# Two chunks of w3 and of w_out per weight tile, and tiles moved by 32 bytes, in a fused attention and two-MLP kernel

## The chip, the cores and the metric

The kernel runs on one core of a Trainium2 chip. The metric is the device time of one execution in microseconds (us). Three executions before the change took 1218.69, 1219.29 and 1219.76 us; the median, 1219.29 us, is what the change is measured against.

## The reference

Attention with four batches, eight heads, 768 positions and head size 64, where a position sees the first 8 keys and the last 96; its result goes through two MLPs without a pause:

```python
scores = scale * np.matmul(q, k.transpose(0, 1, 3, 2))
scores = np.where(keep, scores + bias, -1e9)       # keep: local 96 or global 8
a = softmax(scores); x = np.matmul(a, v)           # -> x: 3072 x 512
h = ((x @ w1) * (x @ w2)) @ w3                     # 512 -> 1024 -> 1024
x = h @ w_out                                      # -> 512
h = x @ w_in                                       # 512 -> 2048
out = (h * np.cos(h)) @ w_out2                     # -> 3072 x 512
```

All of it is float32. The weights reach the device as 8-byte words that the kernel has to decode.

## The kernel before

**Three stages.** First, w3 and w_out are multiplied into one matrix W = w3 @ w_out, in 16 slots `c` (two halves `h`, eight chunks `k`). Second, eight blocks `j` of 384 tokens run attention, up (`up`: x by w1 and by w2) and down (`down`: the product by W), in twelve slots each. Third, six steps `J` of 512 tokens run the second MLP: `hidden` (x by w_in), `gate` (h cos h) and `project` (by w_out2), sixteen chunks `m` per step.

**Order.** It is written by hand (`manual_schedule`): every engine runs its instructions in the order of the code, and waits by semaphores where a tile is not ready or not free.

**Decoding.** Each chunk of 128x512 weights is loaded as `raw` by SyncE, turned into float by ScalarE (`dec_words`: one pass into the chunk's tile, one into `s`), and put together by VectorE (`dec_shift`, `dec_sign`, `dec_sum`). A chunk of w3 or w_out is decoded straight into a tile of the pool `wts`, under the tag `Wb` (four buffers) for w3 and `wB` (eight) for w_out. A buffer there has 4096 bytes per partition, since later tiles (`W`, `wA`, `wB`: a high and a low part of 512 floats) need that much; a chunk fills 2048 of them. In the profile the chunks are `w` and `wo`.

**A slot of the first stage** interleaves the chunk's four matmuls (`wmm`, L835) with attention of unit `n = c - 2`: scores (L529), values of unit n - 2 (`x_ps`, L621), transposes of unit n - 1 (`pt_ps`, L594 and L596), their copy by ScalarE (`pt`, L604 or L609), which the values of the next slot read, the exponentials (`e`, L568), and decoding steps in between. ScalarE's order in a slot is: a chunk of w3 (`w`, `s`), the copy `pt`, other decoding, the exponentials.

**Matmuls of the second and third stage** are made of three: the high part of the stationary operand by the high and by the low part of the moving one, then the low part by the high one (`mm3`, L384 to L386). Each one loads its stationary operand anew. In a name such as `mm<-xT,wA` the moving tile stands first, the stationary one second.

```python
nc.tensor.matmul(ps, lhsT=l_hi, rhs=r_hi, start=first and i == 0, stop=False)
nc.tensor.matmul(ps, lhsT=l_hi, rhs=r_lo, start=False, stop=False)
nc.tensor.matmul(ps, lhsT=l_lo, rhs=r_hi, start=False, stop=last and i == n - 1)
```

The moving operand has 384 columns in `up` and `down` (`xT` by `wA` or `wB`; `ab` by `W`), 512 in `hidden` (`x2in` in even steps J, `x2in_b` in odd ones, by chunks of w_in in `wA`, `wB`, `wC`) and 512 in `project` (chunks of w_out2 in `wB`, `Wa`, `Wb`, and for the last two chunks `wD`, by `g`). Scores of later units (L537, L541) have 232 columns: per head, the stationary q of `hh` by k of `hh` and by the low part `kl`; the second head's k and `kl` begin 928 bytes behind the first one's.

**Where tiles begin.** Pools on the left side grow from low addresses, those on the right side down from the end of a partition. The program's allocation puts the tiles that matmuls read at these bytes of a partition, modulo 512 (all further steps inside a tile are multiples of 512, save the 928 above and 256 in `v`):

| tile | side | before | after |
|---|---|---|---|
| `W`, `wA`, `wB`, `Wa`, `Wb`, `wC`, `x2in` | left | 192 | 192 |
| `hh` (two buffers) | left | 448, 256 | 448, 256 |
| `kl` (two buffers), behind `st` | left | 224, 32 | 320, 128 |
| `pt`, behind `st` | left | 288 | 384 |
| `v` | left | 64 | 64 |
| `xT`, `ab`, `g`, `x2in_b`, `wD` | right | 480 | 448 |

Before, three `st` tiles of 16 bytes, 32 apart, push what follows them on the left by 96 bytes, and the right side ends 32 bytes off a multiple of 64. So before, all tiles of the right side and `kl` and `pt` begin at 32 modulo 64, the rest at 0.

Of the kernel before, what the change touches and what calls it, by code (L numbers as in the profile page):

```python
# [8 lines left out]
F32 = mybir.dt.float32  # L9
# [253 lines left out]
def fused(ctx, tc, a_qk, a_v, w3p, wo1p, w1p, w2p, winp, wo2p, n_global, n_local, out):  # L263
    nc = tc.nc

    def pool(name, bufs, side="left", space=None):
        kw = {} if space is None else {"space": space}
        if space is None:
            kw["side"] = side
        return tc.alloc_tile_pool(name=name, bufs=bufs, reuse_waits="tile", **kw)  # L270
# [2 lines left out]
    x2s = dram.tile([MO, 128, 2, NT], F32R, name="x2s")  # L273
    late_w = dram.tile([2, M2, 128, 512], F32, name="late_w")

    misc = pool("misc", 1)
    wts = pool("wts", 8)
    attn = pool("attn", 2)
# [14 lines left out]

    raws, xs, ss, wt = {}, {}, {}, {}

    rings, taken = {}, {}

    def ring(key, tag, shape, dt):  # L300

        pools = rings[key][tag]
        i = taken[tag] = taken.get(tag, -1) + 1
        at = i % sum(n for _, n in pools)
        for p, n in pools:
            if at < n:
                return p.tile(shape, dt, tag=tag, name=tag, bufs=n)
            at -= n
# [5 lines left out]
    def dec_words(key):  # L314
        r = raws[key]
        if key[0] in ("w3", "wo1"):
            tag = dest[key]
            kw = {"bufs": 4} if tag == "Wb" else {}
            x = xs[key] = wts.tile([128, 512], F32, tag=tag, name=key[0], **kw)
        else:  # L320
            x = xs[key] = ring(key, "x", [128, 512], F32)
        nc.scalar.activation(x, r[:, :, 1].bitcast(F32), ACTF.Copy, scale=2.0 ** -112)
        ss[key] = ring(key, "s", [128, 512], I32)
        nc.scalar.activation(ss[key], r[:, :, 0].bitcast(U32), ACTF.Copy, scale=2.0 ** -29)
# [147 lines left out]
    def where(n):  # L472
        j, r = divmod(n, UPB)
        p, i = divmod(r, TPB)
        return j, p, i, (TPB * j + i) % (S // 128)

    plain = {}
    qk_raw, v_raw, hh, kl, es, sts, pts, xps, xT = {}, {}, {}, {}, {}, {}, {}, {}, {}
# [67 lines left out]
    def a_max(n):  # L546

        if not 0 <= n < NU:
            return
        _, p, _, t = where(n)  # L550
        w = WIN if t else 128
        bias = bias1 if t else bias0
        es[n] = attn.tile([128, 2, WIN], F32, tag="e", name="e", bufs=2)
        sts[n] = attn.tile([128, 2, 2], F32, tag="st", name="st", bufs=3)
        sp = s_ps.pop(n)
        for e in range(2):
            nc.vector.tensor_tensor_reduce(  # L557
                out=es[n][:, e, :w], in0=sp[:, e, :w], in1=bias[:, 2 * p + e, :],
                scale=-0.125, scalar=3.0e38, op0=ALU.add, op1=ALU.min,
                accum_out=top[:, n, e:e + 1],  # L560
            )
# [170 lines left out]
    with tc.manual_schedule():  # L732
# [8 lines left out]
        for o in "3A3A3A3A3A3A3A3ABBBBBBBB":  # L741
# [3 lines left out]
            else:  # L745
                n, m = ups.pop(0)
# [16 lines left out]
        def decoder():  # L763
# [5 lines left out]
            for i in range(n + 5):  # L769
# [13 lines left out]
                if k[0] and fast:  # L783
                    dec_words(k[0])
# [20 lines left out]
                if k[0] and not fast:  # L805
                    dec_words(k[0])
# [22 lines left out]
        for c, (h, k) in enumerate(chunks):  # L829
            n = c - 2  # L830
# [25 lines left out]
            if n >= 0:  # L856
                a_load_plain(n + 2)
            a_values(n - 2)
            a_max(n)
            decode(1)  # L860
            a_out(n - 2)
# [21 lines left out]
        w2p_ = None  # L883
# [7 lines left out]
        for j in range(NB1):  # L891
            for i in range(UPB):
                sl = j * UPB + i
                n = sl + LEAD
                last = j == NB1 - 1
                if last and i == 0:
                    attn.release()
                    w2p_ = pool("w2p", 6)
# [14 lines left out]
                if 1 <= i <= M1:  # L913
                    up_mult(j, i - 1)
                    up_hi(j, i - 1)
                a_max(n)
                decode(3 if sl < 8 else sl % 2)
                if i == 0 and j > 0:
# [34 lines left out]
        p2 = pool("p2", 2, side="right")  # L953
        p_h = pool("p_h", 4, space=PSUM)
        p_o = pool("p_o", 4, space=PSUM)
# [15 lines left out]
        def gate(J, m, meanwhile=iter(())):  # L971
            ps = h_ps.pop((J, m))
            kt = p2.tile([128, TB2], I32, tag="kt", name="kt")
            r = p2.tile([128, TB2], F32, tag="r", name="r")
            nc.scalar.activation(kt, ps, ACTF.Identity, scale=INV2PI)  # L975
            next(meanwhile, None)
            nc.vector.scalar_tensor_tensor(  # L977
                out=r, in0=kt, scalar=-C1, in1=ps, op0=ALU.mult, op1=ALU.add
            )
            nc.vector.scalar_tensor_tensor(  # L980
                out=r, in0=kt, scalar=-C2, in1=r, op0=ALU.mult, op1=ALU.add
            )
            next(meanwhile, None)
            nc.scalar.activation(r, r, ACTF.Sin, scale=0.5)  # L984
            run(meanwhile)
            nc.vector.scalar_tensor_tensor(  # L986
                out=r, in0=r, scalar=-2.0, in1=r, op0=ALU.mult, op1=ALU.mult
            )
            nc.vector.scalar_tensor_tensor(  # L989
                out=r, in0=r, scalar=1.0, in1=ps, op0=ALU.add, op1=ALU.mult  # L990
            )
            t = g[J, m] = p2.tile([128, 2, TB2], F32R, tag="g", name="g", bufs=3)
            nc.scalar.copy(out=t[:, 0, :], in_=r)  # L993
            nc.vector.tensor_tensor(  # L994
                out=t[:, 1, :], in0=r, in1=t[:, 0, :].bitcast(F32), op=ALU.subtract
            )
# [25 lines left out]
        for s in range(len(steps) + LAG):  # L1022
# [14 lines left out]
            if s < len(steps):  # L1037
                if J == 0 and m < 5:
                    tag = ("Wa", "Wa", "Wb", "Wb", "wD")[m]
                    gate(J, m, late_split("o2", 3 + m, tag, p2 if m == 4 else None))  # L1040
                else:
                    gate(J, m)
        for p in (p_o, p_h, p2, w2p_, wts):
            p.release()


# [78 lines left out]
```

## Time and profile before

| | before |
|---|---|
| median of three executions | 1219.29 us |
| the profiled execution | 1223.8 us |
| its span, first to last instruction | 1222.0 us |
| TensorE (PE) busy | 1169.2 us, 96% |
| weight loads (PEld) busy | 988.9 us, 81% |
| VectorE (DVE) busy | 770.5 us, 63% |
| ScalarE (ACT) busy | 579.0 us, 47% |
| mean granted TensorE clock | 0.986 |

Busy times are shares of the whole span, and the three stages differ: the rows further down give stretches. Ends of matmuls are modelled, so that a matmul's pace is read from the distance between the starts of two, not from its duration.

### The profile page before, as it was taken

What the parts mean: (1) busy time and instruction counts of PE and PEld (TensorE: products, weight loads), DVE (VectorE), ACT (ScalarE), POOL (GpSimd) and SP (SyncE); (2) the same over time, 40 slices, a digit from 0 to 9 for tenths busy, and PEclk for the clock granted to TensorE, in tenths of its full rate; (3) what the DMA queues carried; (4) which work ended last, traced back from release to release, by engine and by line L of the source; (5) the groups of instructions that cost most, each with busy time, mean ns of one, the idle gap of its engine ahead of it and who ended that gap; (6) DMA issues with size and microseconds to landing.
All of it is one profiled execution on the core that took longest, in us unless ns stands there. A gap on an engine that the chain in (4) does not pass through costs nothing.

```text
span 1222.0 us, 17352 instructions
## 1 busy us (share of the span) xinstructions
PE 1169.2 (96%) x6178; PEld 988.9 (81%) x6178; DVE 770.5 (63%) x1756; ACT 579.0 (47%) x1256; POOL 124.3 (10%) x213
## 2 busy tenths in 40 slices
PE   4889789999999999999999999999999999999997
PEld 1334678999999999999999888878888888888885
DVE  7578987666667654555534566666666666665664
ACT  5457766666666555555534433333333333333332
POOL 0000122111111111111114200000000000000000
PEclk8889999999999999999999999999999999999998
DMA  8646578565464423334146321201102002000001
GB/s 251 206 153 213 189 267 266 167 186 190 136 214 156 152 87 121 109 100 123 45 138 202 109 68 28 77 1 48 57 1 69 35 1 70 35 1 21 15 1 37
DMA packets 65295, 132.72 MB, mean 109 GB/s; under 512 B 6576, under 2 KB 27184, under 8 KB 65200
## 3 DMA queue, kind: packets, MB, share of 16 engines
q1 hardware_dynamic: 58672, 118.95, 30.3%
q0 software_dynamic: 6528, 12.58, 3.5%
q8 instruction: 50, 0.82, 0.3%
q14 instruction: 45, 0.37, 0.1%
HBM read 104.25 MB, written 27.26 MB: 108 GB/s over the span
## 4 chain that ended last, share of the span: by engine, by line
PE 87%; DVE 4%; ACT 3%; DMA 3%; issue 2%; POOL 0%; SPq 0%; ACTq 0%; DVEq 0%; POOLq 0%
PE mm L384 11%; PE mm L385 10%; PE mm L386 10%; PE o_ps L386 7%; PE o_ps L384 7%; PE h_ps L384 7%; PE h_ps L386 7%; PE o_ps L385 7%; PE h_ps L385 7%; PE x_ps L621 4%; PE mm L835 3%; PE pt_ps L594 2%; PE s_ps L541 1%; PE s_ps L537 1%; PE pt_ps L596 1%
## 5 line engine op out<-in xcount | busy, mean ns | idle before, releaser
L585 POOL TENSOR_SCALAR e<-e,st 128x232 f32<-128x232 f32 (+1 forms) x164 | 84.0, 525 | 528.7 <-DVE st L581 181.0
L984 ACT ACTIVATE r<-r 128x512 f32<-128x512 f32 x96 | 60.7, 632 | 153.5 <-DVE r L980 153.5
L993 ACT CAST g<-r 128x512 fp32r<-128x512 f32 x96 | 59.6, 621 | 139.5 <-DVE r L989 139.5
L505 ACT CAST hh<-qk 128x720 fp32r<-128x720 f32 x82 | 65.0, 793 | 117.2 <-PE s_ps L541 104.7
L986 DVE SCALAR_TENSOR_TENSOR r<-r 128x512 f32<-128x512 f32 x96 | 66.5, 692 | 70.5 <-ACT r L984 70.4
L994 DVE TENSOR_TENSOR g<-r,g 128x512 fp32r<-128x512 f32 x96 | 66.5, 693 | 66.0 <-ACT g L993 66.0
L384 PE MATMUL mm<-xT,wA 128*128 128x384 f32 x256 | 92.3, 361 | 0.0
L384 PE MATMUL mm<-xT,wB 128*128 128x384 f32 x256 | 92.0, 360 | 0.0
L384 PE MATMUL mm<-ab,W 128*128 128x384 f32 x256 | 91.5, 358 | 0.1
L568 ACT ACTIVATE e<-e,top 128x232 f32<-128x232 f32 (+1 forms) x192 | 89.3, 467 | 3.7 <-DVE top L557 3.7
L557 DVE CUSTOM_DVE_ANT_0 e<-s_ps,bias 128x232 f32<-128x232 f32 (+1 forms) x192 | 65.4, 377 | 38.5 <-PE s_ps L541 36.1
L977 DVE SCALAR_TENSOR_TENSOR r<-kt,h_ps 128x512 f32<-128x512 int32 x96 | 65.7, 684 | 33.5 <-ACT kt L975 33.4
L385 PE MATMUL mm<-xT,wA 128*128 128x384 f32 x256 | 86.8, 339 | 0.0
L386 PE MATMUL mm<-xT,wB 128*128 128x384 f32 x256 | 86.8, 339 | 0.0
L386 PE MATMUL mm<-xT,wA 128*128 128x384 f32 x256 | 86.7, 339 | 0.0
L385 PE MATMUL mm<-xT,wB 128*128 128x384 f32 x256 | 86.7, 339 | 0.0
L385 PE MATMUL mm<-ab,W 128*128 128x384 f32 x256 | 86.2, 337 | 0.2 <-DVE ab L671 0.2
L386 PE MATMUL mm<-ab,W 128*128 128x384 f32 x256 | 86.1, 336 | 0.0
L621 PE MATMUL x_ps<-pt,v 128*64 128x128 f32 (+1 forms) x704 | 59.8, 286 | 25.2 <-ACT pt L604 20.5
L835 PE MATMUL mm<-wo,w 128*128 128x512 f32 x128 | 70.1, 681 | 12.8 <-DVE wo L340 12.8
L664 DVE TENSOR_TENSOR ab_f<-mm,a_sb 128x384 f32<-128x384 f32 x64 | 35.6, 556 | 68.0 <-PE mm L386 65.3
L975 ACT ACTIVATE kt<-h_ps 128x512 int32<-128x512 f32 x96 | 57.3, 596 | 39.6 <-PE h_ps L386 39.6
(189 smaller groups left out, 3032.3 us busy)
## 6 DMA issues: line engine op xcount, KB each, us to landing
qk<-in_a_qk SPq DMA_DIRECT2D x82, 360.0 KB, 3.2
v<-in_a_v SPq DMA_DIRECT2D x97, 128.0 KB, 2.1
x2s<-x2t SPq DMA_DIRECT2D x32, 384.0 KB, 3.0
raw<-in_w3p SPq DMA_DIRECT2D x16, 512.0 KB, 4.5
raw<-in_winp SPq DMA_DIRECT2D x16, 512.0 KB, 4.3
late_w<-x SPq DMA_DIRECT2D x32, 256.0 KB, 2.2
raw<-in_wo2p SPq DMA_DIRECT2D x16, 512.0 KB, 4.1
raw<-late_w SPq DMA_DIRECT2D x16, 512.0 KB, 4.6
```

Of the source, the lines that this page charges most:

```text
L384: nc.tensor.matmul(ps, lhsT=l_hi, rhs=r_hi, start=first and i == 0, stop=False)
L385: nc.tensor.matmul(ps, lhsT=l_hi, rhs=r_lo, start=False, stop=False)
L386: nc.tensor.matmul(ps, lhsT=l_lo, rhs=r_hi, start=False, stop=last and i == n - 1)
L505: nc.scalar.copy(out=hh[n], in_=qk_raw[n])
L557: nc.vector.tensor_tensor_reduce(out=es[n][:, e, :w], in0=sp[:, e, :w], in1=bias[:, 2 * p + e, :], scale=-0.125, scalar=3.0e38, op0=ALU.ad ...
L568: nc.scalar.activation(es[n][:, e, :w], es[n][:, e, :w], ACTF.Exp, bias=top[:, n, e:e + 1], scale=-1.0, accum_out=sts[n][:, 0, e:e + 1],)
L585: (engine or nc.gpsimd).tensor_scalar(es[n][:, e, :w], es[n][:, e, :w], st[:, 1, e:e + 1], 1.0, ALU.mult, ALU.mult)
L621: nc.tensor.matmul(x[e * 64:(e + 1) * 64, i * 128:(i + 1) * 128], lhsT=vt[:kk, c, e * 64:(e + 1) * 64], rhs=pt[:kk, e, c, :], start=c == 0 ...
L835: nc.tensor.matmul(W_ps[m], lhsT=wt["w3", c][:, m * 128:(m + 1) * 128], rhs=wt["wo1", k], start=k == 0, stop=k == M1 - 1,)
L977: nc.vector.scalar_tensor_tensor(out=r, in0=kt, scalar=-C1, in1=ps, op0=ALU.mult, op1=ALU.add)
L986: nc.vector.scalar_tensor_tensor(out=r, in0=r, scalar=-2.0, in1=r, op0=ALU.mult, op1=ALU.mult)
L994: nc.vector.tensor_tensor(out=t[:, 1, :], in0=r, in1=t[:, 0, :].bitcast(F32), op=ALU.subtract)
```

## The change

Two edits. Chunks 2i and 2i + 1 of w3, and of w_out, become the two halves of one tile of 4096 bytes. And two tiles are made larger or added for their size alone: `st` grows from 16 to 64 bytes, and a pool `edge` takes 32 bytes at the end of the right side, so that all tiles in the table above begin at multiples of 64 bytes.

```diff
+    edge = pool("edge", 1, side="right")
+    edge.tile([128, 8], F32, name="edge")
     misc = pool("misc", 1)
     wts = pool("wts", 8)
...
         if key[0] in ("w3", "wo1"):
             tag = dest[key]
             kw = {"bufs": 4} if tag == "Wb" else {}
-            x = xs[key] = wts.tile([128, 512], F32, tag=tag, name=key[0], **kw)
+            if key[1] % 2 == 0:
+                two[key[0]] = wts.tile([128, 2, 512], F32, tag=tag, name=key[0], **kw)
+            x = xs[key] = two[key[0]][:, key[1] % 2, :]
...
-        sts[n] = attn.tile([128, 2, 2], F32, tag="st", name="st", bufs=3)
+        sts[n] = attn.tile([128, 8, 2], F32, tag="st", name="st", bufs=3)
```

No instruction changes its place on any engine; what changes is what some of them wait for. On ScalarE, in the slots where the first scores are already under way (`w` is a chunk of w3, `wo` one of w_out; a wait named PE is for a matmul, DMA for a load), it reads before:

```order
31 L322 ACTIVATE w_320<-raw 128x512 [waits DMAHW4_49,PE_49]
32 L324 ACTIVATE s<-raw 128x512 [waits DVE_49,Activation_49]
33 L568 ACTIVATE e,st<-e,top 128x232 [waits DVE_49] x2
34 L609 COPY pt<-pt_ps 128x2x128
35 L322 ACTIVATE wo_355<-raw 128x512 [waits DMAHW7_49]
36 L324 ACTIVATE s<-raw 128x512 [waits Activation_49]
37 L322 ACTIVATE w_367<-raw 128x512 [waits DMAHW0_49,PE_49]
```

The same place after the change (the code stands seven lines further down):

```order
31 L329 ACTIVATE w_275<-raw 128x512 [waits DMAHW4_49]
32 L331 ACTIVATE s<-raw 128x512 [waits DVE_49,Activation_49]
33 L575 ACTIVATE e,st<-e,top 128x232 [waits DVE_49] x2
34 L616 COPY pt<-pt_ps 128x2x128 [waits PE_49]
35 L329 ACTIVATE wo_306<-raw 128x512 [waits DMAHW7_49]
36 L331 ACTIVATE s<-raw 128x512 [waits Activation_49]
37 L329 ACTIVATE w_363<-raw 128x512 [waits DMAHW0_49]
```

The wait for a matmul is gone from the chunks of w3, twelve of the sixteen having had one; the copy `pt` now names its own wait for the transposes, which the chunk ahead of it used to cover.

## Rows read from the trace of the kernel before

**Rows 1.** Windows: length, busy us of each engine (instructions), granted clock, DMA share, GB/s.

```profile
20.00:103.00 83.00, 64.98 (x208) 31.03 (x206) 57.32 (x176) 44.77 (x105) 0.00 (x0) 0.88 0.61 185
103.00:210.00 107.00, 94.11 (x556) 78.28 (x556) 92.40 (x244) 78.23 (x180) 17.07 (x22) 0.97 0.73 242
210.00:678.60 468.60, 468.38 (x3101) 444.27 (x3100) 265.97 (x790) 256.95 (x642) 85.32 (x157) 1.00 0.45 143
678.60:1211.00 532.40, 532.40 (x2300) 430.65 (x2299) 339.83 (x506) 186.71 (x310) 20.68 (x25) 1.00 0.11 35
```

**Rows 2.** Waits, 30 to 104 us: us in total, times, longest.

```profile
ACT w L322 <- PE mm L835: 30.0, 10, 5.2
...
DVE st L578 <- ACT e L568: 12.9, 4, 4.7
...
PE x_ps L621 <- ACT pt L604: 7.7, 5, 2.7
...
PE x_ps L621 <- ACT pt L609: 4.6, 3, 2.4
```

**Rows 3.** Chain that ended last, inside one slot: start, length, what.

```profile
88.80 1.73 PE mm L835 x4
...
90.56 0.70 ACT w L322
91.25 0.56 ACT s L324
91.82 0.26 ACT pt L609
...
92.12 0.44 PE x_ps L621 x4
```

**Rows 4.** Timeline, PE, hidden with x2in: third and last matmul of twelve.

```profile
885.33 0.39 PE L386 MATMUL h_ps<-x2in,wA 128*128 128x512 f32 x1
...
887.37 0.40 PE L386 MATMUL h_ps<-x2in,wA 128*128 128x512 f32 x1
```

**Rows 5.** The same with x2in_b; first of hidden, first and last of project.

```profile
962.41 0.39 PE L384 MATMUL h_ps<-x2in_b,wC 128*128 128x512 f32 x1
...
965.21 0.40 PE L384 MATMUL o_ps<-wB,g 128*128 128x512 f32 x1
...
967.78 0.40 PE L386 MATMUL o_ps<-wB,g 128*128 128x512 f32 x1
```

**Rows 6.** The same, project with wD: two starts six matmuls apart.

```profile
1208.65 0.39 PE L386 MATMUL o_ps<-wD,g 128*128 128x512 f32 x1
...
1210.01 0.39 PE L386 MATMUL o_ps<-wD,g 128*128 128x512 f32 x1
```

**Rows 7.** Timeline, PE: second and last of twelve in down, then one unit's scores.

```profile
400.34 0.34 PE L385 MATMUL mm<-ab,W 128*128 128x384 f32 x1
...
402.07 0.34 PE L386 MATMUL mm<-ab,W 128*128 128x384 f32 x1
402.25 0.27 PE L537 MATMUL s_ps<-hh 128*128 128x232 f32 x1
402.35 0.28 PE L541 MATMUL s_ps<-kl,hh 128*128 128x232 f32 x1
402.46 0.27 PE L537 MATMUL s_ps<-hh 128*128 128x232 f32 x1
402.58 0.27 PE L541 MATMUL s_ps<-kl,hh 128*128 128x232 f32 x1
```

**Rows 8.** Windows of two whole steps: J = 2 with x2in, J = 3 with x2in_b.

```profile
851.73:940.14 88.41, 88.41 (x386) 72.07 (x384) 56.08 (x82) 30.19 (x51) 2.84 (x5) 1.00 0.12 36
940.14:1029.61 89.47, 89.47 (x385) 72.07 (x384) 56.05 (x82) 30.18 (x51) 2.85 (x5) 1.00 0.12 36
```

**Rows 9.** Groups of PE, 210 us to the end: one of nine alike.

```profile
L385 PE MATMUL mm<-xT,wA 128*128 128x384 f32 x224 | 75.4, 336 | 0.0
```

**Rows 10.** One window at the lower granted clock in the first stage.

```profile
44.80:48.20 3.40, 3.40 (x9) 1.74 (x8) 3.17 (x10) 0.10 (x1) 0.00 (x0) 0.50 0.79 241
```

More of the change, by code (lines that the diff above doesn't have):

```diff
@@ L288, in fused @@
     pt_ps = p_t.tile([128, 2, 2, 128], F32, name="pt_ps")
-    raws, xs, ss, wt = {}, {}, {}, {}
+    raws, xs, ss, wt, two = {}, {}, {}, {}, {}
     rings, taken = {}, {}
@@ L1042, in fused @@
                     gate(J, m)
-        for p in (p_o, p_h, p2, w2p_, wts):
+        for p in (p_o, p_h, p2, w2p_, wts, edge):
             p.release()
```

## The prediction

> **What bounds the kernel now.** I read the windows of the stages first, then the waits of the first stage, then the distances between matmul starts in the other two. In [rows 1] TensorE is busy for 468.38 of 468.60 us in the second stage and for all of 532.40 us in the third, at the full granted clock: from 210 us to the last matmul it is the bound, and what counts there is how far apart it starts its matmuls. From 103 to 210 us VectorE, with 92.40 of 107 us, is the fullest; TensorE waits at times. From 20 to 103 us nobody is full: TensorE 64.98 of 83 us, VectorE 57.32, ScalarE 44.77. There the reader should see a ring. ScalarE waits 30.0 us, ten times, with a chunk of w3 for a matmul (L835) to free the buffer [rows 2]. Behind that chunk stand, on ScalarE, `s` and then the copy `pt`, for which the values of the next attention unit wait: the chain runs from four matmuls (1.73 us) through `w` (0.70), `s` (0.56) and `pt` (0.26) back to TensorE [rows 3]. TensorE's idle time before the values, put down to `pt`, is 7.7 + 4.6 = 12.3 us, and VectorE's before `st`, put down to the exponentials that also stand behind the chunk, 12.9 us [rows 2].
>
> **The change: chunks in pairs.** Four buffers hold eight chunks instead of four, so a chunk no longer waits for the matmuls of the chunk four before it; all ten waits go. Nothing is added to any engine. ScalarE then runs the chunk as soon as its load has landed. Most that this can give is the 12.3 us in which TensorE stands still for it, since its remaining time in the stretch is work. What is late next? VectorE: it is busy 57.32 of 83 us, and inside a slot the exponentials wait for its maxima and the transposes for its normalised rows. TensorE's 65 us and VectorE's 57 us must interleave in order, slot by slot, and a slot holds about 5.5 us of either; with 18 us of slack for TensorE to begin with, I do not expect all of it back. Bounds: 2 us, if VectorE or the loads take the place of nearly every wait, and 12.3 us; to the upper one may come the clock: a mean of 0.88 over 83 us [rows 1] means some 20 us at 1.2 GHz, in pieces such as the 3.4 us at 0.50 of [rows 10], and if half of those 20 us ran at 2.4 GHz where TensorE stands still less, that would give back up to 5 us more. I take 9 us, nearer to the upper bound, because VectorE, which is next in line, itself stood 12.9 us for the same exponentials [rows 2] and comes forward with them. From 103 us VectorE bounds the same work in the same order, so the 9 us arrive there early and stay early.
>
> **The change: beginnings.** The trace of before already has both cases. With `x2in`, which begins at 192 like its stationary chunks, nine distances take 887.37 - 885.33 = 2.04 us, 226.7 ns each [rows 4]. With `x2in_b`, at 480 against 192, twelve take 965.21 - 962.41 = 2.80 us, 233.3 ns each; and in `project`, with the moving chunk at 192 and the stationary `g` at 480, eleven take 2.57 us, 233.6 ns [rows 5]. It isn't the 480 as such: with `wD` and `g`, both at 480, six take 1.36 us, 226.7 ns again [rows 6]. So what costs is that the two operands differ by 32 modulo 64: 6.6 to 6.9 ns a matmul of 512 columns. Two whole steps say the same: with 192 matmuls of the matching kind instead of the other, J = 2 is 89.47 - 88.41 = 1.06 us shorter than J = 3, 5.5 ns each [rows 8].
>
> After the change all these tiles begin at 0 modulo 64. Third stage: 576 matmuls of `hidden` on `x2in_b` (3 steps, 16 chunks, 12 each) and 1008 of `project` (6 steps, 14 chunks, 12 each; the two chunks in `wD` already match). At 6.2 ns, between the 5.5 of whole steps and the 6.9 of inner distances, that is 1584 x 6.2 = 9.8 us.
>
> Second stage: six groups of 224 and three of 228 matmuls of 384 columns stand after 210 us [rows 9], 2028 in all, every one with its moving tile (`xT`, `ab`) at 480 against 192; none of this width matches anywhere, so its price is bounded. One run has ten distances in 402.07 - 400.34 = 1.73 us, 173 ns [rows 7]; over the stage the inner distances average 174.6 ns. Below: scores of 232 columns, first head, match, and go 0.10 us to the next [rows 7] (105 ns over 81 units); the straight line from there to 226.7 ns at 512 columns gives 105 + 152 x 0.435 = 171 ns at 384, a gain of 3.5 ns (nothing but 2 ns if that one run were typical). Above: the 6.6 ns of 512 columns, and where 232 columns do not match the next start is 0.11 to 0.12 us off (112 and 113 ns over the units), 7 to 8 ns more, so the loss doesn't shrink with width. I take 5 ns, between the two: 10.1 us, with 4 to 13.4 for the range. The 276 earlier ones stand where VectorE is the bound and count nothing.
>
> Scores: `kl` of the first head now matches (82 units by 7 ns, 0.6 us gained); `kl` of the second head, 928 bytes on, matched before and no longer does, but what follows it is not another such matmul but the values, which wait for their own copy, so I cost that at nothing; if it counts, it takes the 0.6 us back. The larger `st` and the new pool move no instruction and add none.
>
> At this place a rule speaks against the change. The Trainium skill, "TensorE: Matmul & The Clock Gate", section "Step-by-step: what each phase is for", says that TensorE has two independent read ports, one for the moving operand and one for weight loads, so that loading the next weights takes nothing from the running matmul. By it no beginning could matter and this part's gain would be nothing; rows 4 to 6, at 226.7 against 233.6 ns, disagree. The trace decides, and I give the rule's outcome to a rival below.
>
> **The sum.** 9 + 9.8 + 10.1 + 0.6 = 29.5 us. The profiled execution took 1223.8 us (span 1222.0), so it would take 1194.3; the median of the three runs lies 4.5 us under the profiled one, and I forecast a median of **1190 us**.
>
> **Rivals.** (1) Beginnings pay, pairs don't: ScalarE's wait for the matmul is replaced by one for a load or for VectorE. For it: VectorE is busy for 57.32 us of 83, the DMA share is 0.61, and loads stand in SyncE's queue behind loads of `v` that wait for the values. Against: VectorE itself waited for the exponentials. 20.5 us without the 9, of which 2 may stay: 1197 to 1199 us. (2) Pairs pay, beginnings don't: the offset that costs is not 32 but any difference below 512, and after the change the right side still stands 256 off the left one (448 against 192). Every pair that was slow had the 32 in its difference, every fast one had a difference of 0, so the trace has no pair that is 256 off alone. Against: differences of 288 and of 224 (rows 5) cost the same within 0.3 ns, so the larger bits seem to do nothing. 1219.3 - 9, 1210 us. The rule of the Trainium skill quoted above, from "TensorE: Matmul & The Clock Gate", would give the same time. (3) Neither: 1219 us, within 0.2%, which is about what a measurement of this kernel can tell from no change. (4) Slower: 256 off costs more than 32 did. It would bite in the second and third stage, at some 3600 matmuls; from 2.5 ns on top of today's each it outweighs the 9 us of the pairs, and at twice today's loss (6.6 more, 3612 x 6.6 = 24 us) the time is 1234 us. Against it stands the same 0.3 ns.
>
> **Chances and range.** Both parts pay, 1181 to 1198 us: 0.70. Rival 1: 0.12. Rival 2: 0.12. Rival 3: 0.03. Rival 4: 0.03. The forecast's own bounds: least 2 + 8.7 + 4 = 15 us (1584 x 5.5 = 8.7), most 12.3 + 10.9 + 13.4 + 0.6 + 5 for the clock = 42; both ends at once are unlikely, and 1180 to 1206 us holds rival 1 and most of the first case, with a little of rival 2: 8 in 10. Faster by over 0.2%: 0.94; same: 0.03; slower: 0.03.
>
> **What would show it.** Pairs: ScalarE's wait for L835 before a chunk of w3 gone from the waits; TensorE's idle time before the values between 20 and 103 us down from 12.3 to about 3 us; the second stage's full part beginning 9 us sooner. Beginnings: a step J of 87.3 us, odd or even; 226.7 ns inside runs of `hidden` and of `project`; about 169 to 170 ns inside `up` and `down`. Wrong it would be if the distances stay at 233 and 174 ns (the 256), if ScalarE stands before the same chunks for another releaser, or if TensorE, quicker by 3%, begins to stop in the second stage for VectorE, which has 266 of 468.6 us of work there.

## The result, and the profile after

Four executions of the changed kernel took 1187.69 to 1192.95 us, median **1191.43 us**, beside 1218.99 us (1217.78 to 1219.76) for the kernel before on the same chip: a ratio of 0.977, 95% interval 0.9746 to 0.9794. The forecast said 1190 us. The profiled execution took 1191.22 us, its span is 1189.4 us, 32.6 us below that of before; by medians the gain is 27.6 us, since the profiled execution of before stood 4.8 us over the median given here and the one of after does not. What follows compares the two profiled executions.

Line numbers are higher by seven in after (L842 for L835, L391 to L393 for L384 to L386). The windows of the stages, with the columns of [rows 1] and the borders moved to where the third stage now begins:

```profile
20.00:103.00 83.00, 78.17 (x294) 38.90 (x293) 75.79 (x229) 60.77 (x140) 0.00 (x0) 0.96 0.78 246
...
210.00:657.40 447.40, 446.79 (x2960) 423.49 (x2959) 250.92 (x745) 243.61 (x610) 81.32 (x149) 1.00 0.45 140
657.40:1189.00 531.60, 523.42 (x2307) 431.98 (x2305) 340.54 (x508) 187.57 (x312) 20.73 (x25) 1.00 0.12 37
```

Between 20 and 103 us TensorE is now busy for 78.17 us where it was for 64.98, and has 294 instructions where it had 208; VectorE's 57.32 us have become 75.79. The stretch in which nobody was full is full. The waits of 30 to 104 us, as in [rows 2]:

```profile
ACT e L575 <- DVE top L564: 6.3, 10, 1.8
ACT pt L611 <- PE pt_ps L603: 4.0, 3, 1.8
...
ACT w L329 <- DMA raw<-in_w3p: 1.1, 2, 0.8
```

ScalarE's 30.0 us for a matmul before a chunk of w3 are gone, and 1.1 us for loads of w3 stand there. TensorE has no wait left in these 74 us that is put down to anything, where it had 12.3 us before the values and 0.7 before transposes. The last values of the first part, and the first matmul of `up` behind them, before and then after:

```profile
127.87 0.66 PE L621 MATMUL x_ps<-pt,v 128*64 128x128 f32 x8 [2.17 <-ACT pt L604]
128.46 0.45 PE L384 MATMUL mm<-xT,wA 128*128 128x384 f32 x1
```

```profile
107.59 0.66 PE L628 MATMUL x_ps<-pt,v 128*64 128x128 f32 x8 [2.18 <-ACT pt L611]
108.18 0.44 PE L391 MATMUL mm<-xT,wA 128*128 128x384 f32 x1
```

So 20.3 us have been gained when the second stage's matmuls begin; the wait of 2.2 us for `pt` right before these values stands in both. Stops make 13.0 us of the gain. The rest shows in the granted clock. First three windows of before, at half the clock beside the one of [rows 10], then two of after, which together cover the stretch from 24.80 us to the values above:

```profile
24.30:34.50 10.20, 7.18 (x11) 3.40 (x12) 6.99 (x22) 2.47 (x4) 0.00 (x0) 0.50 1.04 296
...
68.70:72.10 3.40, 3.40 (x8) 1.52 (x7) 2.96 (x9) 0.29 (x1) 0.00 (x0) 0.50 0.69 200
...
79.00:82.40 3.40, 3.40 (x9) 1.74 (x8) 3.40 (x12) 1.47 (x4) 0.00 (x0) 0.50 0.72 207
```

```profile
24.80:31.60 6.80, 4.34 (x7) 2.34 (x8) 5.20 (x20) 3.34 (x6) 0.00 (x0) 0.50 1.03 344
31.60:107.50 75.90, 73.81 (x290) 37.07 (x288) 69.95 (x209) 59.46 (x142) 0.00 (x0) 1.00 0.75 240
```

Before, 10.2 + 3 x 3.4 = 20.4 us passed at 1.2 GHz, after 6.8. The 13.6 us between them count at most half, 6.8 us, since the same work takes half as long at 2.4 GHz. 13.0 + 6.8 = 19.8 of the 20.3 us. TensorE's busy time from 20 us to the first `up` agrees: 88.28 us before, 81.17 after, 7.1 less.

Not all of the 6.8 us belongs to the ring. The first stretch at half the clock, 10.2 us before and 6.8 after, begins while TensorE waits for a load of `hh` (5.07 us before, 4.83 after), which neither edit touches. The three of 3.4 us each that lie among the stops are worth 5.1 us at most.

The third stage, in two whole steps as in [rows 8], J = 2 and J = 3:

```profile
826.89:913.93 87.04, 87.04 (x385) 72.07 (x384) 55.97 (x82) 30.21 (x51) 2.85 (x5) 1.00 0.12 37
913.93:1000.97 87.04, 87.04 (x385) 72.07 (x384) 55.99 (x82) 30.21 (x51) 2.85 (x5) 1.00 0.12 37
```

The same step took 88.41 and 89.47 us; odd and even are now alike. Inside them, as in [rows 5]: `project` with its first and last matmul of twelve, then `hidden` with `x2in_b`.

```profile
911.21 0.39 PE L391 MATMUL o_ps<-Wb,g 128*128 128x512 f32 x1
...
913.71 0.39 PE L393 MATMUL o_ps<-Wb,g 128*128 128x512 f32 x1
913.93 0.39 PE L391 MATMUL h_ps<-x2in_b,wC 128*128 128x512 f32 x1
...
916.65 0.39 PE L391 MATMUL o_ps<-wD,g 128*128 128x512 f32 x1
```

Eleven distances in 2.50 us and twelve in 2.72 us, 227 and 226.7 ns, where there were 233.6 and 233.3. The first matmul of `hidden` and the last of `project`, before and then after:

```profile
678.67 0.40 PE L384 MATMUL h_ps<-x2in,wC 128*128 128x512 f32 x1
...
1212.76 0.39 PE L386 MATMUL o_ps<-wD,g 128*128 128x512 f32 x1
```

```profile
657.37 0.39 PE L391 MATMUL h_ps<-x2in,wC 128*128 128x512 f32 x1
...
1180.43 0.40 PE L393 MATMUL o_ps<-wD,g 128*128 128x512 f32 x1
```

From one to the other the stage takes 523.1 us instead of 534.1: 11.0 us less.

The second stage has gained next to nothing. Timeline of TensorE, as in [rows 7]: second and last matmul of a `down`, then one unit's scores.

```profile
390.66 0.34 PE L392 MATMUL mm<-ab,W 128*128 128x384 f32 x1
...
392.40 0.34 PE L393 MATMUL mm<-ab,W 128*128 128x384 f32 x1
392.57 0.27 PE L544 MATMUL s_ps<-hh 128*128 128x232 f32 x1
392.68 0.28 PE L548 MATMUL s_ps<-kl,hh 128*128 128x232 f32 x1
392.79 0.28 PE L544 MATMUL s_ps<-hh 128*128 128x232 f32 x1
392.91 0.27 PE L548 MATMUL s_ps<-kl,hh 128*128 128x232 f32 x1
```

Ten distances in 1.74 us are 174 ns, as before the change (1.73 us). The unit's first and last start are 0.34 us apart, before 0.33. From the first `up` to the first `hidden` it is 549.2 us, before 550.2. That 1.0 us is no more than the spread: the kernels below whose differences are 0 or 256 bytes, as in after, take 547.9 to 550.6 us. The inner distances at 384 columns average 174.5 ns before and 174.1 after, which over 2028 matmuls is 0.7 us. 20.3 + 1.0 + 11.0 = 32.3 us, the gain of the span to within 0.3 us.

### The profile page after: what moved, and what is told of

It is laid out like the page before. It is cut to its first block, busy times and chain, and to the rows that moved or that the text cites. A ratio compares the mean times of both kernels' runs of the same rounds, so it can differ in the third digit from the quotient of the medians.

```text
span 1189.4 us, 17345 instructions
## 1 busy us (share of the span) xinstructions
PE 1151.1 (97%) x6178; PEld 985.5 (83%) x6178; DVE 769.1 (65%) x1756; ACT 579.6 (49%) x1256; POOL 124.9 (10%) x213
## 5 line engine op out<-in xcount | busy, mean ns | idle before, releaser
L391 PE MATMUL mm<-ab,W 128*128 128x384 f32 x256 | 91.8, 358 | 0.5 <-ACT ab L675 0.5
L391 PE MATMUL mm<-xT,wA 128*128 128x384 f32 x256 | 91.7, 358 | 0.0
L391 PE MATMUL mm<-xT,wB 128*128 128x384 f32 x256 | 91.1, 356 | 0.0
L393 PE MATMUL mm<-xT,wA 128*128 128x384 f32 x256 | 86.9, 339 | 0.0
L393 PE MATMUL mm<-ab,W 128*128 128x384 f32 x256 | 86.6, 338 | 0.0
L393 PE MATMUL mm<-xT,wB 128*128 128x384 f32 x256 | 86.1, 336 | 0.0
L842 PE MATMUL mm<-wo,w 128*128 128x512 f32 x128 | 64.9, 637 | 12.7 <-DVE wo L347 12.7
```

The costliest lines, as they stand in the source:

```text
L842: nc.tensor.matmul(W_ps[m], lhsT=wt["w3", c][:, m * 128:(m + 1) * 128], rhs=wt["wo1", k], start=k == 0, stop=k == M1 - 1,)
```

## The experiments

Eight kernels were timed, four at a time on one chip, beside the kernel before: its median was 1219.27 us beside pairs alone, beginnings alone, 192 and no difference, 1220.87 us beside the other four. The ninth was executed once, with the profiler.

**Pairs alone.** After without its filler pool and with the small `st`, so that every tile of the second and third stage begins where it did before:

```diff
-    edge = pool("edge", 1, side="right")
-    edge.tile([128, 8], F32, name="edge")
-        sts[n] = attn.tile([128, 8, 2], F32, tag="st", name="st", bufs=3)
+        sts[n] = attn.tile([128, 2, 2], F32, tag="st", name="st", bufs=3)
```

> The chunks in pairs alone, all tiles beginning where they did before. Theory A, from the two traces: the pairs are worth about 20 us, since all 13 us of TensorE's stops between 27 and 107 us go and some 6.6 us come from the clock; the beginnings are worth 11 us and only in the third stage. Then this kernel takes about 1199 us, its third stage begins near 658 us and lasts 534 us as before, and matmuls of 512 columns keep 233 ns where they had it. Theory B, the sizes of the forecast (pairs 9 us, beginnings 20.5 us): 1210 us.

1200.64 us (1199.89 to 1201.99), ratio 0.984, interval 0.9816 to 0.9864: 18.6 us by medians, twice the term of the forecast. The stretch up to the values, in a window, and J = 3:

```profile
31.90:107.50 75.60, 73.43 (x293) 37.06 (x293) 69.20 (x208) 58.52 (x137) 0.00 (x0) 1.00 0.74 239
...
919.01:1008.48 89.47, 89.47 (x385) 72.05 (x384) 56.14 (x82) 30.28 (x51) 2.85 (x5) 1.00 0.12 36
```

The full clock from 31.90 us on and the missing stops come with the pairs alone, and J = 3 takes to the hundredth what it took before; the third stage takes 534.1 us. The two edits act in different stages.

**Beginnings alone.** Before with the filler pool and the large `st`:

```diff
+    edge = pool("edge", 1, side="right")
+    edge.tile([128, 8], F32, name="edge")
-        sts[n] = attn.tile([128, 2, 2], F32, tag="st", name="st", bufs=3)
+        sts[n] = attn.tile([128, 8, 2], F32, tag="st", name="st", bufs=3)
```

> The beginnings alone (larger st, 32 bytes at the end of the right side), chunks one to a buffer as before. Theory A: 1208 us, third stage 523 us with 226.7 ns throughout, first two stages as long as before (third stage begins near 678 us), 384 columns at 174 ns. Theory B: 1198.5 us, with the third stage beginning near 668 us.

1206.77 us (1204.64 to 1211.47), ratio 0.9897, interval 0.9861 to 0.9933: 12.5 us. The third stage takes 523.1 us, 11.0 less than before; it begins at 674.1 us and not near 678, since the first `up` starts at 125.52 us, 2.9 sooner than before. The waits of 30 to 104 us, and the windows at half the clock:

```profile
ACT w L324 <- PE mm L837: 28.2, 10, 5.3
...
PE x_ps L623 <- ACT pt L606: 7.7, 5, 2.7
PE x_ps L623 <- ACT pt L611: 4.6, 3, 2.4
```

```profile
27.40:30.80 3.40, 3.40 (x5) 1.49 (x5) 2.62 (x12) 1.23 (x2) 0.00 (x0) 0.50 1.03 399
41.00:44.40 3.40, 3.40 (x8) 1.52 (x9) 3.40 (x12) 1.08 (x2) 0.00 (x0) 0.51 0.71 243
51.30:54.70 3.40, 3.40 (x8) 1.73 (x7) 2.30 (x8) 0.00 (x0) 0.00 (x0) 0.50 0.78 241
75.20:78.60 3.40, 3.40 (x12) 1.52 (x9) 3.40 (x11) 2.30 (x5) 0.00 (x0) 0.50 0.43 99
```

With the wait for the matmul there are again 12.3 us of stops and three falls of the clock after 31 us, as many as before but not at the same times. The first stretch at half the clock, the one beside the load of `hh`, lasts 3.4 us here and 10.2 before; half of those 6.8 us covers the 2.9 us by which `up` comes sooner, so that part differs between executions with the same stops. Between 33 and 107 us the granted clock is 0.92 in before, 0.93 here, and 1.00 in all nine kernels with the pairs. So the three falls go with the stops, though which stop brings which fall is not shown. By medians the two edits alone add up to 18.6 + 12.5 = 31.1 us beside the 27.6 of both together, whose interval, 25.1 to 31.0, all but reaches it.

**Pairs for w3 alone.** After, with a tile for each chunk of w_out again:

```diff
+            if key[0] == "wo1":
+                x = xs[key] = wts.tile([128, 512], F32, tag=tag, name=key[0], **kw)
+            else:
+                if key[1] % 2 == 0:
+                    two[key[0]] = wts.tile([128, 2, 512], F32, tag=tag, name=key[0], **kw)
+                x = xs[key] = two[key[0]][:, key[1] % 2, :]
```

> The kernel after with the pairs for the chunks of w3 alone; each chunk of wo1 has a tile of its own again, as before. Theory A: the stops that the pairs removed were those on w3's chunks, which take the buffers first; the eight chunks of wo1 add no wait that TensorE meets: 1191 us, first three-term matmul at about 108 us. Theory B: the pairs pay through the number of tiles in the ring, and half of them bring half: TensorE meets some 6 us of stops again before 107 us, first three-term matmul at 114 to 118 us, 1198 to 1201 us.

1190.6 us (1189.23 to 1192.55), ratio 0.9755, interval 0.974 to 0.977; first `up` at 108.1 us. ScalarE's wait before a chunk of w3 is one for loads, and short:

```profile
ACT w L332 <- DMA raw<-in_w3p: 1.7, 3, 0.6
```

The ring of w3 was the whole of it, as far as these times tell; the pairs of w_out add nothing to be seen.

**A difference that is a multiple of 64, but not of 256.** The change was made for multiples of 64; by the tiles' table it leaves the right side 256 bytes off the left. These three kernels keep every tile at a multiple of 32 or 64 and move the right side alone:

```diff
-    edge.tile([128, 8], F32, name="edge")
+    edge.tile([128, 24], F32, name="edge")
```

> The change with 96 instead of 32 bytes at the end of the right side and the small st: right-side tiles begin at 384 modulo 512, so they differ from the left ones by 192, a multiple of 64 but not of 256. If multiples of 64 are what counts: third stage 523 us, 226.7 ns at 512 columns, time 1191 us as after the change. If only multiples of 256 are free of loss, as the scores of 232 columns after the change hint (difference 384: 114.6 ns, difference 0: 104 ns): 233 ns, third stage 534 us, about 1202 us.

(here `st` is the small one again.) 1197.76 us (1197.29 to 1198.45), ratio 0.9821, interval 0.9796 to 0.9845. J = 2 and 3:

```profile
827.98:915.52 87.54, 87.54 (x386) 72.11 (x384) 56.06 (x82) 30.18 (x51) 2.83 (x5) 1.00 0.12 37
915.52:1004.74 89.22, 89.22 (x386) 72.14 (x385) 56.13 (x82) 30.34 (x51) 2.90 (x5) 1.00 0.12 36
```

For the other two `edge` has 40 and 56 columns, and `flag_rows`, 512 bytes on the left side, moves to another pool:

```diff
-    edge.tile([128, 8], F32, name="edge")
+    edge.tile([128, 40], F32, name="edge")
-        m = misc.tile([4, 128], F32, name="flag_rows")
+        m = w2p_.tile([4, 128], F32, name="flag_rows", bufs=1)
```

> The kernel after with its filler tile on the right widened from 8 to 40 columns, and flag_rows (512 B) moved to another pool: the tiles of the right side now begin at 320 (modulo 512 bytes), the weights of the left side at 192, so that the two operands of a 512-column matmul differ by 128 in hidden and project. Known so far: differences 0 and 256 cost nothing (226.7 ns), 192 costs (233.4 ns), 320 half (230.4 ns). Theory A, the free step is 256 bytes: 128 costs like 192, third stage about 530 us, 512-column distances of 230 to 234 ns, about 1198 us. Theory B, the free step is 128 bytes: 226.7 ns, third stage 523 us, 1191 us.

1204.13 us (1202.95 to 1205.95), ratio 0.9867, interval 0.9852 to 0.9882, slower than expected too. J = 2 and 3:

```profile
831.10:919.77 88.67, 88.67 (x385) 72.22 (x384) 56.05 (x82) 30.22 (x51) 2.85 (x5) 1.00 0.12 36
919.77:1009.11 89.34, 89.34 (x386) 72.10 (x384) 56.15 (x82) 30.34 (x51) 2.86 (x5) 1.00 0.12 36
```

> The same with a filler tile of 56 columns: the right side at 256 modulo 512 bytes, the left at 192, a difference of 64. If an odd multiple of 64 costs whatever the size (192 did), the third stage is about 530 us long and the kernel takes about 1198 us. If only the larger differences cost and a small one is nearly free, 226.7 ns, 523 us and 1191 us.

1198.89 us (1198.23 to 1201.0), ratio 0.9817, interval 0.9802 to 0.9832. J = 3:

```profile
918.53:1007.58 89.05, 89.05 (x385) 72.14 (x384) 56.14 (x82) 30.28 (x51) 2.84 (x5) 1.00 0.11 36
```

All three have the pairs, and lose most or all of the third stage's gain: 530.6 (192), 534.5 (128) and 533.4 us (64) for it against 523.1. The rule that I had read out of [rows 4 to 6], 32 modulo 64, is wrong: 64, 128 and 192 bytes cost as well. The sign of a difference counts, since `hidden` has the right side as its moving operand and `project` as its stationary one: 192 bytes give 233.4 ns in `hidden` with `x2in_b` and 230.4 in `project`, which has -192, or 64 modulo 256; 64 bytes give 231.3 and, with -64 or 192 modulo 256, 233.6. That is why 192 lies between its two expectations.

At 64 and 128 bytes `hidden` with `x2in` is slower too, 229 ns as a mean, though its own operands agree: a run of twelve starts with some seven distances of 224 to 236 ns and then goes on at 227. That its neighbours' difference costs it this start fits the series of 256 and 512 bytes further down, which start the same way; it was not tested by itself.

That 128 bytes take 5 to 6 us longer than the other two is the third stage in part (1 to 4 us) and the second stage in part (about 2 us; 384 columns have a mean distance of 175.8 ns there, at 64 bytes 173.2). Against 192 bytes this is all of the 5.6 us between the profiled spans; against 64 bytes the spans differ by 1.9 us only, and the rest of the medians' 5.2 I have not traced.

**No difference at all.** `edge` of 72 columns and `flag_rows` moved put both sides at 192:

```diff
-    edge.tile([128, 8], F32, name="edge")
+    edge.tile([128, 72], F32, name="edge")
-        m = misc.tile([4, 128], F32, name="flag_rows")
+        m = w2p_.tile([4, 128], F32, name="flag_rows", bufs=1)
```

> The change with 288 bytes at the end of the right side (room for it comes from one 512-byte tile of the flags that is kept in another pool): all matmul tiles of both sides begin at 192 modulo 512, so the difference is 0 and no longer 256. If the 256 still costs the matmuls of 384 columns what the forecast thought they lose (some 5 ns of 174), the second stage gets 10 us shorter: 1181 us. If matmuls of 384 columns have hardly a loss to give back, as theory A has it: 1191 us, 173 to 174 ns.

1190.62 us (1190.52 to 1191.08), ratio 0.976, interval 0.9736 to 0.9784; J = 2 and 3 take 87.04 us, and the mean distance of 384 columns is 174.1 ns, as in after. 256 bytes of difference cost nothing to be seen, and 384 columns have nothing more to give back.

**The scores.** The second head's k moved to a multiple of 512 bytes behind q, `kl` sized to match, `st` small, and small tiles moved so that all differences are 0 or 256:

```diff
+KS = 256
+QK_W = 2 * 128 + KS + WIN
-        kl[n] = attn.tile([128, 2 * WIN], F32R, tag="kl", name="kl")
+        kl[n] = attn.tile([128, KS + WIN], F32R, tag="kl", name="kl")
...
-                s_ps[n][:, e, :], lhsT=q, rhs=l[:, e * WIN:(e + 1) * WIN],
+                s_ps[n][:, e, :], lhsT=q, rhs=l[:, e * KS:e * KS + WIN],
```

> The kernel after with the second head's k at column 512 of the tile of q and k (it was at 488), so that k begins a multiple of 512 bytes behind q for both heads, kl sized to match, and with five small tiles and four of the scalars' tiles moved so that weights, hh, kl and the right side differ by 0 or 256 bytes everywhere. Theory A, what holds for the 512 columns (difference 0 or 256 costs nothing, 384 and 416 cost) holds for the scores' 232 columns: the three distances per unit of 113 to 115 ns fall to 104 to 105 ns, 3 x 82 x 10 ns = 2.5 us, about 1189 us; third stage still 523 us. Theory B, the scores' extra ns come from something else (the first head's 112 ns did not fall with the alignment to 64): no change, 1191 us.

1190.58 us (1189.18 to 1192.51), ratio 0.9752, interval 0.9739 to 0.9765: as after, so not a better kernel. The three distances of a unit were 104, 115 and 115 ns in after, as means over the units, and are 107, 110 and 114 here, not 104 to 105 each. The beginnings shift ns from one to the other and give back 3 ns a unit, 0.2 us in all.

**The operands by themselves.** Behind the last `project` of after, 32 series of 24 matmuls on a tile no longer used; nothing else runs on the other engines to speak of, and nobody reads the result, which the output does not contain:

```diff
+        flat = x2in[4].rearrange("p a b c -> p (a b c)")
+        def series(cols, at, stationary=(0, 128)):
+            ps = p_h.tile([128, TB2], F32, tag="h", name="h_ps")
+            for i in range(24):
+                s = stationary[i % 2]
+                nc.tensor.matmul(
+                    ps[:, :cols], lhsT=flat[:, s:s + 128],
+                    rhs=flat[:, 1024 + at:1024 + at + cols], start=i == 0, stop=i == 23,
+                )
```

> The kernel after with 32 series of 24 matmuls each behind its last project (some 0.15 ms more), all on one tile that is no longer used (x2in of J = 4), so that only the beginnings of the two operands change; nobody reads their result. In the first 17 series (512 columns) the stationary chunks begin at 0 modulo 512 bytes and the moving operand 0, 8, 16, 32, 64, 96, 128, 160, 192, 224, 256, 288, 320, 384, 448, 480 and 512 bytes further. Theory A, what costs is the difference modulo 256 bytes: 226.7 ns at 0, 256 and 512, 230 to 234 ns at all others, the first 8 and 16 bytes unknown. Theory B, the price belongs to the tiles or to what else the third stage does: 226.7 ns in all. Next, stationary chunks that alternate between differences of 0 and 128: if the price comes from reading the moving columns while the next weights are read, the distance is long (233 ns) where the next chunk differs, and 226.7 ns where the matmul's own does; if from its own operands, the reverse. Both chunks shifted by 128: 233 ns all along. The same chunk all along, shifted by 128: 226.7 ns if no weights are read again, 233 ns if they are. Then 384, 232 and 128 columns at differences of 0, 32, 128 and 192: by what is known 173 to 175 ns at 384 for all four; at 232 columns 104 ns at 0 and 112 to 115 ns at the others if the scores' distances come from this, 104 to 109 ns for all if not.

Windows from the start of one series to that of the next (length, busy us of TensorE, granted clock, DMA share, GB/s; the counts take in neighbours at the edges). A length over 24 is the mean distance. Differences of 0, 8, 32, 64, 128, 256 and 512 bytes at 512 columns, in this order:

```profile
1180.26:1185.70 5.44, 5.44 (x25) 1.00 0.46 168
1185.70:1191.31 5.61, 5.61 (x25) 1.00 0.01 3
...
1196.87:1202.47 5.60, 5.60 (x25) 1.00 0.00 0
1202.47:1207.96 5.49, 5.49 (x25) 1.00 0.01 3
...
1213.58:1219.17 5.59, 5.59 (x25) 1.00 0.00 0
...
1235.99:1241.46 5.47, 5.47 (x26) 1.00 0.01 3
...
1269.33:1274.80 5.47, 5.47 (x26) 1.00 0.00 0
```

226.7 ns at 0; at 256 and 512 five distances of 228 to 236 ns and then 226.7. 229 ns at 64 and at 320. All others, 8 and 16 bytes too, take 232 to 234 ns as means. Theory A holds with one step between. Then the stationary chunks that alternate between differences of 0 and 128, and one and the same chunk at 128; then 384 columns at 0 and 128, 232 columns at 0 and 128, and 128 columns at 0:

```profile
1274.80:1280.40 5.60, 5.60 (x25) 1.00 0.00 0
...
1285.98:1291.55 5.57, 5.57 (x25) 1.00 0.00 0
1291.55:1295.73 4.18, 4.18 (x25) 1.00 0.01 4
...
1299.89:1304.12 4.23, 4.23 (x26) 1.00 0.00 0
...
1308.31:1310.98 2.67, 2.67 (x25) 1.00 0.00 0
...
1313.67:1316.35 2.68, 2.68 (x26) 1.00 0.02 6
...
1319.05:1321.68 2.63, 2.63 (x26) 1.00 0.00 0
```

The alternating chunks settle nothing: all the distances inside the series are 232 to 235 ns, behind either chunk, which neither theory had expected. The same chunk again and again costs as much. At 384 columns the four differences give 173 to 176 ns, the most at 128 bytes, 2 ns above no difference, as in the kernel with 128; 232 columns give 111 to 113 whatever the difference, and 128 columns 110 to 112 as well: at these two widths the distance hardly depends on the beginnings, nor on the number of columns.

## Why the prediction came true, point by point

**The sum.** 29.5 us were forecast and 32.3 came in the profiled executions, 27.6 by medians. The total was right by luck: two terms were wrong by nearly the same amount in opposite directions, the pairs 11.3 us too low and the second stage 9.1 too high.

**Pairs: 9 us, measured 20.3** (18.6 by medians, pairs alone). The mechanism was right: the ring's wait goes, nothing takes its place. Mis-sized was "I do not expect all of it back". I had VectorE late next, because the two engines' work had to interleave; all 13.0 us of stops went, VectorE was busy for 18 us more of the same 83, and TensorE with it. The clock came on top with up to 6.8 us, 5.1 of them among the stops, where I had allowed up to 5 and taken none. Both parts came out at or above my upper bounds (12.3 and 5), the stops because I had left out the 0.7 us before transposes; what failed was the choice of a point well below the bounds. The stops and those 5.1 us make 18.1 us, near the 18.6 by medians. VectorE's own 12.9 us of waiting, which I named as the reason to go up, was the better guide. I had named 3 us of stops as what would remain before the values between 20 and 103 us; none did. Rival 1, a load in place of the matmul, is out: ScalarE waits 1.1 us in all for loads of w3 in that stretch, 0.8 at most, and the pairs alone pay 18.6 us.

**Third stage: 9.8 us, measured 11.0.** Right. 1584 matmuls by the 6.9 ns of inner distances are 10.9 us. The 5.5 ns from the difference of two whole steps, which pulled my middle down, understated it, because both steps paid and J = 2 paid more for each: 88.41 - 87.04 = 1.37 us for its 168 slow matmuls of `project`, 8.2 ns each, where J = 3 paid 2.43 us for 168 + 192, 6.75 ns each.

**Second stage: 10.1 us, measured 1.0** (0.7 by the distances). This step failed. It took a loss of 5 ns at 384 columns from two rows that were no bound on it: a straight line through 232 columns, and 112 to 113 ns at 232 read as a loss of 7 to 8. The operands by themselves show 173 to 176 ns at 384 columns with all four differences tried, and about 112 at 232 with all four and at 128 columns too, so 232 columns say next to nothing of the beginnings. The run of ten at 173 ns [rows 7] was typical, and no beginning made it shorter: the lowest mean of any kernel is 173.2 ns. I had it as the lower bound. The 169 to 170 ns that were to show the gain are the mean of no kernel and of no series.

**Scores: 0.6 us, measured none.** The first head's `kl` matched by my rule but differs by 384 bytes, and its distance went from 112 to 115 ns; full agreement gave 0.2 us.

**The rule, 32 modulo 64.** Wrong, though the forecast survived it. The change works because 448 against 192 happens to be 256; rival 2's premise, that other differences cost as well, is nearly true, and its conclusion for this change is false by that accident. Had the filler been 24, 40 or 56 columns, every tile it moves would still begin at a multiple of 64, and the third stage would have gained 3.5 us at most. The rows before had differences of 0, 224 and 288 only, and I took two slow differences that cost the same, 224 and 288, as if they chose between rules; modulo 256 they are 32 below and 32 above a multiple. Rival 4, that 256 costs more than 32, is out: without any difference the time is the same, 1190.62 us.

**The Trainium skill's rule.** "TensorE: Matmul & The Clock Gate", section "Step-by-step: what each phase is for", has the moving operand and the weight loads on ports that do not disturb each other. Where nothing but the beginnings changes, the distances are 226.7 and 233 ns, so beginnings do matter; that the two reads collide would fit, but the alternating chunks did not show whose read it is, and it stays open. So does why 384 columns pay next to nothing.

## What to carry to other kernels

When TensorE is the bound, compare the distances of alike matmuls whose operands lie differently; here, with 512 columns of this type, their start addresses had to agree modulo 256 bytes, and one filler tile in the right pool was worth 11 us. Before carrying such a price to another width, find a pair of rows at that width, or measure it: at 384 columns hardly any of it was there. And where a buffer's wait on ScalarE stops TensorE, count what its granted clock may give back on top of the stops (here up to 5.1 us beside 13.0).

## What I had not expected of the hardware

- A moving operand 8 bytes off its stationary chunk costs as much as one 128 bytes off (233 to 234 against 226.7 ns at 512 columns), and 64 or 320 bytes some 40% of it (229 ns).
- Hardly any such price at 384 columns: 173 to 176 ns, with 128 bytes at the upper end.
- 232 and 128 columns start at the same pace, about 112 ns, in a dense run.
- After a change of difference to 256 or 512 the first five distances are still 228 to 236 ns before they settle at 226.7.
